# Four edits to an attention-and-FFN kernel: GpSimd operations in pieces, a tensor_reduce for the sums, an earlier hash at the seams, one transposed copy in four on VectorE

## The chip, the cores and the metric

The kernel runs on one core of a Trainium2 chip. Its engines are TensorE (PE in the profile, with weight loads shown apart as PEld), VectorE (DVE), ScalarE (ACT), GpSimd (POOL) and SyncE (SP, which here only issues DMAs). The metric is the device time of one execution in microseconds (us), lower is better.

## The reference

Four batches of eight heads, 768 positions, 64 features per head, all in 32-bit floats. Positions attend only to positions in the same hash bucket; the result goes through an FFN with a three-tap convolution and a gate.

```python
q_bits = (np.einsum('bhsd,dk->bhsk', q, proj) > 0)        # 6 bits; k_bits likewise
mask = q_bucket[:, :, :, None] == k_bucket[:, :, None, :]
scores = np.where(mask, scale * np.matmul(q, k.transpose(0, 1, 3, 2)), -1e9)
attn = np.exp(scores - max)
attn = attn / (np.sum(attn, axis=-1, keepdims=True) + 1e-09)
x = np.matmul(attn, v)                                    # heads side by side: 512 features
h = np.maximum(x @ w_in, 0.0)                             # 1024 features
gate = 1.0 / (1.0 + np.exp(-conv3(h, conv_w)))
out = h * gate @ w_out
```

## The kernel before, in words

**Units.** Two heads make a pair; 4 batches give 16 pairs. A pair has 12 units, each one head's block of 128 queries, in three blocks `qb` of four units (two query tiles `tq` times two heads `h`). The main loop runs over the units `i` and writes out, for every engine, the work of unit `i` and of older units; each engine then runs its own instructions strictly in that order.

**One turn of the loop.** TensorE makes the scores `s` of unit i (`products`, L286). VectorE takes them from PSUM with the row maximum into `e` (`maximum`, L299) and makes `st` (L303). TensorE transposes the exponentials of unit i-3 into `t` (L329), and ScalarE copies them to `at` (`to_sbuf`, L336) and then does the exponential of unit i (L306). `s`, `t` and the hash share three PSUM slots in turn; so the transposes of unit i-1, which come two turns after its scores do, in turn i+2, wait until the maximum of unit i+1 has read its slot.

**The burst.** Every fourth turn, TensorE also does the 24 matmuls of attention times values of an older block (`v`, L355). In that same turn VectorE scales the block before it (`x`, L364), GpSimd splits that into a high part `xh` (L365) and a low part `xl` (L366), and both take their share of the background work below. In the first six pairs the softmax is normalised after the values, by factors `rec` made from four row sums (`reciprocals`: 1e-9 added at L320, reciprocal at L321, spread at L323). In later pairs GpSimd normalises `e` directly (L314).

**Background work, in the first six pairs.** The weights arrive as 64-bit floats. VectorE decodes 16 blocks of 512 columns with four instructions each: L95, L97 (`upper`), L102, L104 (`lower`). ScalarE rounds the result (L136), and GpSimd makes the low part in `ends` (L139, L140). At each burst 3.75 such VectorE steps are written out. The decoded block lies in one of two buffers `wu`, so L97 of a block waits for the `ends` (L140) of the block two before it.

**Preparing the next pair.** Queries and keys of a pair arrive in one buffer `R`. `split` makes the high part `hi` (L204) and the low part in place (L209, called lo below) and sends both out by DMAs; `hash` multiplies `R` by the projection on TensorE (L219), VectorE makes bits (L222), GpSimd scales them (L224). `prepare` cuts this into seven steps; from the second unit of a pair on, one step is taken per turn. `R` of the pair after the next is loaded at a pair's eighth unit, when its last low part has been sent.

**The FFN.** A batch's FFN runs two pairs after its attention. The turns in which the last block of such a pair is transposed are called `ending`; at the last of them the whole FFN is written out (`ffn`: matmuls `h` L393 and `o` L423, VectorE L402 and L406, GpSimd L412), and it takes prepare's steps from its fourth step on. This place is called the seam; there are three with a pair still to be prepared.

Of the kernel before, what the change touches and what calls it, by code (L numbers as in the profile page):

```python
# [7 lines left out]
F32 = mybir.dt.float32  # L8
# [4 lines left out]
ALU = mybir.AluOpType  # L13

B, H, S, D = 4, 8, 768, 64
NB = 6
DM, DFF = 512, 1024
P = 128
NP = H // 2
NCK = S // P  # L20
HS = S // 2
QB = 256
# [15 lines left out]
W0 = 7  # L38
RATE = 3.75
WC = 512  # L40


@with_exitstack
def lsh_attention_conv_ffn(ctx, tc, qk, v, hw, w_in, conv_w, w_out, consts, ident_in, out):
    nc = tc.nc
    PSUM = bass.MemoryType.PSUM
    cp = ctx.enter_context(tc.tile_pool(name="const", bufs=1))
    wp = ctx.enter_context(tc.tile_pool(name="work", bufs=1))
# [4 lines left out]
    def ring(pool, bufs, shape, dtype, tag, name):  # L53

        k = turns[tag] = (turns.get(tag, -1) + 1) % bufs
        return pool.tile(shape, dtype, tag=f"{tag}{k}", name=name, bufs=1)
# [8 lines left out]
    nc.scalar.dma_start(cst, consts)  # L65

    weights = {}

    Q2s = [cp.tile([96, 2, S], F32R, name=f"q2_{i}") for i in range(2)]
    K2s = [cp.tile([96, 2, S], F32R, name=f"k2_{i}") for i in range(2)]  # L70
# [3 lines left out]
    class Decode:  # L74
# [4 lines left out]
        def __init__(self, raw, n, name):  # L79
            pr, self.name = raw.rearrange("p (n two) -> p n two", two=2), name  # L80
            self.lo, self.hi = pr[:, :, 0].bitcast(U32), pr[:, :, 1]
            self.up, self.low = (ring(wp, bufs, [P, WC], I32, f"w{x}", f"w{x}{name}")[:, :n]
                                for x, bufs in (("u", 2), ("l", 5)))
# [23 lines left out]
    def split_weights():  # L107

        todo, ends = [], None

        def ahead():
            if fetched:
                raw, name = fetched.pop(0)
                todo.append(Decode(raw, WC, name))
                todo[-1].size()

        ahead()  # L120
        ahead()
        yield
        for d in todo:
            d.clamp()
        yield
        while todo:
            d = todo.pop(0)
            ahead()
            yield from d.upper()
            if ends:  # L130
                ends()
            if len(todo) == 2:
                todo[-1].clamp()
            yield from d.lower()
            blk = weights[d.name] = cp.tile([P, 2, WC], F32R, tag=f"w{d.name}", name=f"w{d.name}")
            nc.scalar.copy(blk[:, 0, :], d.upf)  # L136

            def ends(d=d, blk=blk):
                nc.gpsimd.tensor_tensor(d.upf, d.upf, blk[:, 0, :].bitcast(F32), ALU.subtract)  # L139
                nc.gpsimd.tensor_tensor(blk[:, 1, :], d.upf, d.lowf, ALU.add)  # L140

        ends()

    def decode_taps(raw):
# [32 lines left out]
    class Pair:  # L177
# [22 lines left out]
        def split(self, h):  # L200

            lo, R = self.R[:, h], self.R[:, h].bitcast(F32)
            hi = ring(wp, 1, [P, S], F32R, "hi", f"hi{self.nm}_{h}")
            nc.gpsimd.tensor_scalar(hi, R, 1.0, 0.0, ALU.mult, ALU.add)  # L204
            for dst, src in ((self.Q1[:64, h], hi[:64]), (self.Q2[:64, h], hi[:64]),
                             (self.K1[:64, h], hi[64:]), (self.K1[64:, h], hi[64:])):
                nc.sync.dma_start(dst.bitcast(F32), src.bitcast(F32))
            yield
            nc.gpsimd.tensor_tensor(lo, R, hi.bitcast(F32), ALU.subtract)  # L209
            for dst, src in ((self.Q1[64:, h], lo[:64]), (self.K2[:64, h], lo[64:])):  # L210
                nc.sync.dma_start(dst.bitcast(F32), src.bitcast(F32))

# [61 lines left out]
    class Unit:  # L274
# [14 lines left out]
        def maximum(self, prev):  # L289

            self.st = ring(wp, 8, [P, 4], F32, "st", f"st{self.nm}")
            pr = self.pair
            if self.tq == 0 and self.h == 0 and not pr.late:
                pr.sums = ring(wp, 3, [P, QB // P, 2], F32, "sums", f"sums{self.nm}")
            self.sums = None if pr.late else pr.sums
            self.sum = self.st[:, 2:3] if pr.late else pr.sums[:, self.tq, self.h:self.h + 1]
            e = wp.tile([P, 776], F32, tag="e", name=f"e{self.nm}", bufs=EB)
            self.e = e[:, :S]
            nc.vector.tensor_scalar(self.e.rearrange("p (a b) -> p a b", a=2), self.sp[:, :, :HS],  # L299
                                    MASKED, None, ALU.max, ALU.max, accum_out=self.st[:, 0:1])  # L300
            if prev and prev.pair.late:
                prev.total()
            nc.vector.tensor_scalar(self.st[:, 1:2], self.st[:, 0:1], -SCALE, None, ALU.mult)  # L303
# [12 lines left out]
        def reciprocals(self):  # L316

            pr = self.pair
            sums = self.sums
            nc.vector.tensor_scalar(sums, sums, 1e-9, None, ALU.add)  # L320
            nc.vector.reciprocal(sums, sums)  # L321
            pr.rec = ring(wp, 1, [P, QB // P, 2, D], F32, "rec", f"rec{self.nm}")
            nc.gpsimd.tensor_scalar(pr.rec, sums.unsqueeze(3).to_broadcast([P, QB // P, 2, D]), 1.0, 0.0,  # L323
                                    ALU.mult, ALU.add)

        def transposes(self):
# [5 lines left out]
        def to_sbuf(self):  # L332
            pr = self.pair
            if self.tq == 0 and self.h == 0:
                pr.at = [ring(wp, 4, [P, 2, 3, QB], F32, "big", f"at{pr.nm}_{self.qb}_{hh}") for hh in range(2)]
            nc.scalar.copy(pr.at[self.h][:, :, :, self.tq * P:(self.tq + 1) * P],  # L336
                           self.tp[:, :, :3 * P].rearrange("p j (c q) -> p j c q", c=3))

    def values(pr, qb, ats, rec):

# [41 lines left out]
    g2, prep = [None], [iter(())]  # L382
# [94 lines left out]
    n = len(units)  # L477
    ffn_after = {min((b + 1) * NP - 1 + DEFER, B * NP - 1): b for b in range(B)}
    for i in range(n + LAG):
        u = units[i] if i < n else None  # L480
        w = units[i - LAG] if i >= LAG else None
        prev = units[i - 1] if 1 <= i <= n else None
        pi, k = divmod(i, 2 * NCK)
        burst = AVS[(i - LAG) % 4] > 0
        for high, low in outs:
            high()
        lows, outs = lows + outs, []
        wi = (i - LAG) // (2 * NCK)
        ending = w and wi in ffn_after and w.qb == S // QB - 1
        if u:  # L490
            u.products()
        if ending:
            for high, low in lows:
                low()
            lows = []
        if u:
            u.maximum(prev)
        elif prev and prev.pair.late:
            prev.total()
        two = units[i - 2] if 2 <= i <= n + 1 else None  # L500
        if two and not two.pair.late and two.tq == QB // P - 1 and two.h == 1:
            two.reciprocals()
        if w and w is not early:
            w.transposes()
            w.to_sbuf()
        if u:
            u.exponential()
        if prev and prev.pair.late:
            prev.normalise()
        if i in (0, 2):  # L510
            next(first, None)
        if burst:
            for high, low in lows:
                low()
            lows = []
        if u and k == PREP and pi + 1 < len(pairs):
            prep[0] = pairs[pi + 1].prepare()
        next(prep[0], None)
        for _ in range(1 + NCK if ending else AVS[(i - LAG) % 4]):
            if av:  # L520
                steps, last = av[0]
                steps.pop(0)()
                if not steps:
                    outs.append(last)
                    av.pop(0)
        if burst and i >= W0:
            background(RATE)
        if u and k == PREP + PREP_N and pi + 1 < len(pairs):
            pairs[pi + 1].load_v()
            if pi + 2 < len(pairs):  # L530
                pairs[pi + 2].load()
        if i == 3:
            taps.append(decode_taps(cwr))
        for g in taps:
            next(g, None)
        fetch(i % 2 if i < 8 else burst)
        if w and w.tq == QB // P - 1 and w.h == 1:
            if not ending:
                av.append(values(w.pair, w.qb, w.pair.at, w.pair.rec))
            else:  # L540
                def fill():
                    steps, last = values(w.pair, w.qb, w.pair.at, w.pair.rec)
                    for step in [*steps, *last]:
                        step()

                bi = ffn_after[wi]
                early = units[i + 1 - LAG] if i + 1 - LAG < n else None

                def transposes_ahead():
                    if early:  # L550
                        early.transposes()
                        early.to_sbuf()
                        turns["S"] -= 1

                ffn(bi, [pairs[bi * NP + c].x for c in range(NCC)], fill, transposes_ahead)
# [43 lines left out]
```

## Time and profile before

| | |
|---|---|
| median of 3 runs | 749.99 us (748.79 to 753.88) |
| profiled execution, its own time | 750.76 us |
| its span in the trace | 749.0 us |
| mean granted TensorE clock | 0.984 of full speed |
| busy share: PE, DVE, ACT, POOL | 95%, 67%, 68%, 50% |

Busy shares are means over the whole span. In the rows of the profile the columns are: line, engine, operation, out<-in with sizes, count, then busy time, mean duration, and the idle time ahead with what ended it. A timeline row begins with start and duration; the idle time before it stands in brackets.

### The profile page before, as it was taken

What the parts mean: (1) busy time and instruction counts of PE and PEld (TensorE: products, weight loads), DVE (VectorE), ACT (ScalarE), POOL (GpSimd) and SP (SyncE); (2) the same over time, 40 slices, a digit from 0 to 9 for tenths busy, and PEclk for the clock granted to TensorE, in tenths of its full rate; (3) what the DMA queues carried; (4) which work ended last, traced back from release to release, by engine and by line L of the source; (5) the groups of instructions that cost most, each with busy time, mean ns of one, the idle gap of its engine ahead of it and who ended that gap; (6) DMA issues with size and microseconds to landing.
All of it is one profiled execution on the core that took longest, in us unless ns stands there. A gap on an engine that the chain in (4) does not pass through costs nothing.

```text
span 749.0 us, 13385 instructions
## 1 busy us (share of the span) xinstructions
PE 714.4 (95%) x4588; PEld 587.5 (78%) x4588; DVE 499.2 (67%) x1195; ACT 509.2 (68%) x954; POOL 373.6 (50%) x372
## 2 busy tenths in 40 slices
PE   5989999988899999999999999999999999999997
PEld 3767777776679987777788988777788897778986
DVE  7588999977667656666657655665666665564663
ACT  5867887886655548778774557787785547785554
POOL 4366777756566324755735423656645323341221
PEclk8999999998999999999999999999999999999999
DMA  3876576553412102365441302255461211000011
GB/s 141 198 204 155 141 206 181 168 162 85 114 43 72 64 37 70 82 181 136 121 121 31 104 1 105 68 150 132 119 163 33 70 43 63 2 1 1 0 43 43
DMA packets 30357, 72.18 MB, mean 96 GB/s; under 512 B 5937, under 2 KB 7505, under 8 KB 30289
## 3 DMA queue, kind: packets, MB, share of 16 engines
q1 hardware_dynamic: 27696, 62.88, 30.9%
q10 hardware_dynamic: 2592, 8.44, 3.6%
q8 instruction: 37, 0.61, 0.3%
q14 instruction: 32, 0.25, 0.1%
HBM read 27.40 MB, written 6.29 MB: 45 GB/s over the span
## 4 chain that ended last, share of the span: by engine, by line
PE 69%; DVE 4%; POOL 4%; DMA 3%; ACT 1%; issue 1%; SPq 0%; POOLq 0%; DVEq 0%
PE o L423 18%; PE h L393 17%; PE s L286 11%; PE t L329 11%; PE v L355 11%; DVE e L299 2%; DMA k<-R 1%; DMA R<-in_qk 1%; PE hash L219 1%; POOL wuo L139 1%; POOL e L314 1%; POOL wo L140 1%; ACT e L306 1%; DVE wuo L97 1%; POOL R L209 1%
## 5 line engine op out<-in xcount | busy, mean ns | idle before, releaser
L299 DVE TENSOR_SCALAR_CACHE_REDUCE e<-s 128x768 f32<-128x768 f32 x192 | 183.3, 955 | 80.9 <-PE s L286 72.1
L306 ACT ACTIVATE e<-e,st 128x768 f32<-128x768 f32 x192 | 181.2, 944 | 23.1 <-DVE st L303 12.8
L336 ACT COPY at<-t 128x768 f32<-128x768 f32 x192 | 152.3, 794 | 47.3 <-PE t L329 47.1
L329 PE MATMUL t<-ident,e 128*128 128x128 f32 x1152 | 164.5, 280 | 19.9 <-DVE e L299 17.9
L314 POOL TENSOR_SCALAR e<-e,st 128x768 f32<-128x768 f32 x120 | 109.3, 911 | 117.3 <-ACT at L336 59.9
L329 PEld LDWEIGHTS t<-ident,e 128*128 128x128 f32 x1152 | 133.4, 144 | 42.6 <-DVE e L299 22.4
L402 DVE SCALAR_TENSOR_TENSOR ht<-ht,cw 128x384 f32<-128x384 f32 (+1 forms) x128 | 117.8, 921 | 70.0 <-ACT ht L400 66.8
L412 POOL TENSOR_TENSOR g<-ht,g 128x384 fp32r<-128x384 f32 x64 | 72.0, 1125 | 163.9 <-ACT g L411 129.7
L423 PE MATMUL o<-wo,g 128*128 128x512 f32 x576 | 143.3, 395 | 0.7 <-POOL g L412 0.7
L393 PE MATMUL h<-xh,wi 128*128 128x386 f32 x512 | 142.0, 340 | 0.0
L355 PE MATMUL v<-at,v 128*64 128x256 f32 x1152 | 134.9, 383 | 0.0
L423 PEld LDWEIGHTS o<-wo,g 128*128 128x128 f32 x576 | 107.0, 188 | 23.5 <-ACT ht L400 1.2
L286 PE MATMUL s<-K,Q 128*128 128x384 f32 x384 | 118.7, 391 | 1.0 <-POOL K L253 0.9
L355 PEld LDWEIGHTS v<-at,v 128*64 128x64 f32 x1152 | 78.7, 137 | 45.5 <-issue 10.9
L286 PE MATMUL s<-k,q 96*128 96x384 f32 x384 | 102.2, 348 | 2.2 <-DVE e L299 2.2
L405 ACT ACTIVATE ht<-ht 128x384 f32<-128x384 f32 x64 | 33.6, 525 | 96.4 <-DVE ht L402 96.4
L393 PEld LDWEIGHTS h<-xh,wi 128*128 128x128 f32 x512 | 94.0, 188 | 3.7 <-ACT ht L400 1.2
L393 PE MATMUL h<-xl,wi 128*128 128x386 f32 x256 | 86.8, 339 | 0.0
L286 PEld LDWEIGHTS s<-K,Q 128*128 128x128 f32 x384 | 60.1, 196 | 22.2 <-issue 17.4
L286 PEld LDWEIGHTS s<-k,q 96*128 96x128 f32 x384 | 72.9, 197 | 3.0 <-ACT q L266 3.0
L406 DVE TENSOR_TENSOR ht<-ht 128x384 f32<-128x384 f32 x64 | 41.5, 649 | 31.5 <-ACT ht L405 31.3
L209 POOL TENSOR_TENSOR R<-R,hi 128x768 fp32r<-128x768 f32 x30 | 60.4, 2014 | 0.9 <-PE hash L219 0.8
(75 smaller groups left out, 622.2 us busy)
## 6 DMA issues: line engine op xcount, KB each, us to landing
R<-in_qk SPq DMA_DIRECT2D x15, 768.0 KB
K<-hi SPq DMA_DIRECT2D x60, 192.0 KB
v<-in_v SPq DMA_DIRECT2D x16, 384.0 KB
out<-osb SPq DMA_DIRECT2D x24, 256.0 KB
Q<-hi SPq DMA_DIRECT2D x30, 192.0 KB
q<-hi SPq DMA_DIRECT2D x30, 192.0 KB
Q<-R SPq DMA_DIRECT2D x30, 192.0 KB
k<-R SPq DMA_DIRECT2D x30, 192.0 KB
```

The costliest lines, as they stand in the source:

```text
L209: nc.gpsimd.tensor_tensor(lo, R, hi.bitcast(F32), ALU.subtract)
L286: nc.tensor.matmul(self.sp[:, half, :HS], A[:, h, qs], C[:, h, half * HS:(half + 1) * HS], start=(kk == 0), stop=(kk == 1))
L299: nc.vector.tensor_scalar(self.e.rearrange("p (a b) -> p a b", a=2), self.sp[:, :, :HS], MASKED, None, ALU.max, ALU.max, accum_out=self.st ...
L306: nc.scalar.activation(self.e, self.e, AF.Exp, bias=self.st[:, 1:2], scale=SCALE, accum_out=self.sum)
L314: nc.gpsimd.tensor_scalar(self.e, self.e, self.st[:, 3:4], 0.0, ALU.mult, ALU.add)
L329: nc.tensor.transpose(self.tp[:, c // 3, c % 3 * P:(c % 3 + 1) * P], self.e[:, c * P:(c + 1) * P], ident)
L336: nc.scalar.copy(pr.at[self.h][:, :, :, self.tq * P:(self.tq + 1) * P], self.tp[:, :, :3 * P].rearrange("p j (c q) -> p j c q", c=3))
L355: nc.tensor.matmul(av[h * D:(h + 1) * D, :QB], vt[:, c, h, :], ats[h][:, c // 3, c % 3, :], start=(c == 0), stop=(c == NCK - 1), tile_posi ...
L393: nc.tensor.matmul(hp[:, :HW], w, x[:, c0:c0 + HW], start=(n == 0), stop=(n == 3 * NCC - 1))
L402: nc.vector.scalar_tensor_tensor(t[:, a:z], ht[:, o + k - 1 + a:o + k - 1 + z], cw[:, f, k:k + 1], t[:, a:z], ALU.mult, ALU.add)
L412: nc.gpsimd.tensor_tensor(g[:, 1, :], t, g[:, 0, :].bitcast(F32), ALU.subtract)
L423: nc.tensor.matmul(op, l, r, start=(f == 0 and n == 0), stop=(f == NFC - 1 and n == 2))
```

## The change

- **Pieces.** GpSimd's lo (L209) and both instructions of `ends` (L139, L140) are done in pieces of 256 columns, `hi` (L204) in pieces of 384.
- **Sums.** The three buffers of row sums have a second column that GpSimd fills with 1e-9 once at the start. A `tensor_reduce` over the two columns takes the place of the addition at L320.
- **Seam.** In `ending` turns a second step of `prepare` is taken.
- **Copy.** The copy to `at` for the first unit of each block (one in four) is done by VectorE; the others stay on ScalarE.

```diff
+PC = 256
+def pieces(n, step):
+    return [slice(c, c + step) for c in range(0, n, step)]
...
+    sums4 = [cp.tile([P, 2 * QB // P, 2], F32, name=f"sums{i}") for i in range(3)]
+    for t in sums4:
+        nc.gpsimd.memset(t, 1e-9)
...
             def ends(d=d, blk=blk):
-                nc.gpsimd.tensor_tensor(d.upf, d.upf, blk[:, 0, :].bitcast(F32), ALU.subtract)
-                nc.gpsimd.tensor_tensor(blk[:, 1, :], d.upf, d.lowf, ALU.add)
+                for c in pieces(WC, PC):
+                    nc.gpsimd.tensor_tensor(d.upf[:, c], d.upf[:, c], blk[:, 0, c].bitcast(F32), ALU.subtract)
+                for c in pieces(WC, PC):
+                    nc.gpsimd.tensor_tensor(blk[:, 1, c], d.upf[:, c], d.lowf[:, c], ALU.add)
...
-            nc.gpsimd.tensor_scalar(hi, R, 1.0, 0.0, ALU.mult, ALU.add)
+            for c in pieces(S, HS):
+                nc.gpsimd.tensor_scalar(hi[:, c], R[:, c], 1.0, 0.0, ALU.mult, ALU.add)
...
-            nc.gpsimd.tensor_tensor(lo, R, hi.bitcast(F32), ALU.subtract)
+            for c in pieces(S, PC):
+                nc.gpsimd.tensor_tensor(lo[:, c], R[:, c], hi[:, c].bitcast(F32), ALU.subtract)
...
-                pr.sums = ring(wp, 3, [P, QB // P, 2], F32, "sums", f"sums{self.nm}")
+                pr.sums = sums4[self.qb % 3]
...
-            self.sum = self.st[:, 2:3] if pr.late else pr.sums[:, self.tq, self.h:self.h + 1]
+            self.sum = self.st[:, 2:3] if pr.late else pr.sums[:, 2 * self.tq + self.h, 0:1]
...
-            nc.vector.tensor_scalar(sums, sums, 1e-9, None, ALU.add)
-            nc.vector.reciprocal(sums, sums)
+            inv = ring(wp, 2, [P, QB // P, 2], F32, "inv", f"inv{self.nm}")
+            nc.vector.tensor_reduce(inv.rearrange("p t h -> p (t h)"), sums, mybir.AxisListType.X, ALU.add)
+            nc.vector.reciprocal(inv, inv)
...
-            nc.scalar.copy(pr.at[self.h][:, :, :, self.tq * P:(self.tq + 1) * P],
-                           self.tp[:, :, :3 * P].rearrange("p j (c q) -> p j c q", c=3))
+            copy = nc.vector.tensor_copy if self.tq == 0 and self.h == 0 else nc.scalar.copy
+            copy(pr.at[self.h][:, :, :, self.tq * P:(self.tq + 1) * P],
+                 self.tp[:, :, :3 * P].rearrange("p j (c q) -> p j c q", c=3))
...
         next(prep[0], None)
+        if ending:
+            next(prep[0], None)
```

Line numbers move, so the rows of the change carry other numbers than those of before (L299 becomes L312, L364 becomes L380, L95 to L104 become L104 to L113, L139 and L140 become L149 and L151, L209 becomes L222, L219 becomes L232).

VectorE in a burst of the third pair, before (maximum of unit i, its `st`, `x`, four decode steps, maximum of unit i+1):

```order
L299 TENSOR_SCALAR e_2_3_1_1051,st_2_3_1_1050<-s_2_3_1_1045 128x768
L303 TENSOR_SCALAR st_2_3_1_1050<-st_2_3_1_1050 128x1
L364 TENSOR_TENSOR x_1_2_1065<-v_1_2_902,rs_1_2_903 128x256
L95 TENSOR_SCALAR wli_1_717<-wli_1_717 128x512
L97 SCALAR_TENSOR_TENSOR wui_1_716<-rawi_1_586,wli_1_717 128x512
L102 TENSOR_SCALAR wli_1_717<-wui_1_716 128x512
L104 SCALAR_TENSOR_TENSOR wli_1_717<-rawi_1_586,wli_1_717 128x512
L299 TENSOR_SCALAR e_2_4_0_1114,st_2_4_0_1112<-s_2_4_0_1107 128x768
```

And the same place of the changed kernel:

```order
L312 TENSOR_SCALAR e_2_3_1_1080,st_2_3_1_1079<-s_2_3_1_1074 128x768
L316 TENSOR_SCALAR st_2_3_1_1079<-st_2_3_1_1079 128x1
L352 COPY at_2_1_0_1090<-t_2_2_0_1083 128x6x128
L380 TENSOR_TENSOR x_1_2_1094<-v_1_2_926,rs_1_2_927 128x256
L104 TENSOR_SCALAR wli_1_738<-wli_1_738 128x512
L106 SCALAR_TENSOR_TENSOR wui_1_737<-rawi_1_602,wli_1_738 128x512
L111 TENSOR_SCALAR wli_1_738<-wui_1_737 128x512
L113 SCALAR_TENSOR_TENSOR wli_1_738<-rawi_1_602,wli_1_738 128x512
L312 TENSOR_SCALAR e_2_4_0_1146,st_2_4_0_1145<-s_2_4_0_1140 128x768
```

The copy to `at` now stands in VectorE's queue in the burst's turn, ahead of `x`, the decode steps and the next maximum.

GpSimd in the burst of the sixth pair near 184 us, before:

```order
L365 TENSOR_SCALAR xh_0_1808<-x_0_2_2208 128x256
L366 TENSOR_TENSOR xl_0_1809<-x_0_2_2208,xh_0_1808 128x256
L209 TENSOR_TENSOR R_2_1863<-R_2_1863,hi_2_1_2160 128x768
L139 TENSOR_TENSOR wuo_1722<-wuo_1722,wo_2102 128x512
L140 TENSOR_TENSOR wo_2102<-wuo_1722,wlo_1723 128x512
```

And now:

```order
L381 TENSOR_SCALAR xh_0_1861<-x_0_2_2271 128x256
L382 TENSOR_TENSOR xl_0_1862<-x_0_2_2271,xh_0_1861 128x256
L222 TENSOR_TENSOR R_2_1918<-R_2_1918,hi_2_1_2222 128x256 x3
L149 TENSOR_TENSOR wuo_1772<-wuo_1772,wo_2164 128x256 x2
L151 TENSOR_TENSOR wo_2164<-wuo_1772,wlo_1773 128x256 x2
```

The order is the same; three instructions have become seven.

TensorE at the second seam, before (last scores and transposes ahead of the FFN, first FFN matmuls; the hash stood sixty rows further on, ahead of the first `o`):

```order
L286 MATMUL s_2_0_1_4328<-k_0_75,q_0_73 128x384 x2
L329 MATMUL t_1_5_1_4338<-ident,e_1_5_1_4249 128x128 x6
L393 MATMUL h_0_0_4350<-xh_0_1808,wi_0_450 128x386
L393 MATMUL h_0_0_4350<-xl_0_1809,wi_0_450 128x386
L393 MATMUL h_0_0_4350<-xh_0_1808,wi_0_450 128x386
```

And now:

```order
L299 MATMUL s_2_0_1_4427<-k_0_81,q_0_79 128x384 x2
L343 MATMUL t_1_5_1_4437<-ident,e_1_5_1_4347 128x128 x6
L232 MATMUL hash_3_4448<-R_3_4271,hw_sb 32x384 x4
L409 MATMUL h_0_0_4470<-xh_0_1861,wi_0_461 128x386
L409 MATMUL h_0_0_4470<-xl_0_1862,wi_0_461 128x386
```

The hash of the next pair has moved ahead of the FFN's first matmul.

More of the change, by code (lines that the diff above doesn't have):

```diff
@@ L319, in reciprocals @@
             sums = self.sums
-            nc.vector.tensor_scalar(sums, sums, 1e-9, None, ALU.add)
-            nc.vector.reciprocal(sums, sums)
+            inv = ring(wp, 2, [P, QB // P, 2], F32, "inv", f"inv{self.nm}")
+            nc.vector.tensor_reduce(inv.rearrange("p t h -> p (t h)"), sums, mybir.AxisListType.X, ALU.add)
+            nc.vector.reciprocal(inv, inv)
             pr.rec = ring(wp, 1, [P, QB // P, 2, D], F32, "rec", f"rec{self.nm}")
-            nc.gpsimd.tensor_scalar(pr.rec, sums.unsqueeze(3).to_broadcast([P, QB // P, 2, D]), 1.0, 0.0,
+            nc.gpsimd.tensor_scalar(pr.rec, inv.unsqueeze(3).to_broadcast([P, QB // P, 2, D]), 1.0, 0.0,
                                     ALU.mult, ALU.add)
```

## The prediction

> **What bounds the kernel now.** The page comes first, then the busy times by stage, then TensorE's waits in each stage.
>
> ```profile
> span 749.0 us, 13385 instructions
> PE 714.4 (95%) x4588; PEld 587.5 (78%) x4588; DVE 499.2 (67%) x1195; ACT 509.2 (68%) x954; POOL 373.6 (50%) x372
> ```
> ```profile
> 24.70:155.00 130.30, 119.30 (x873) 93.81 (x872) 112.22 (x240) 102.16 (x191) 90.02 (x91) 0.97 0.63 173
> 155.00:204.90 49.90, 41.81 (x281) 33.80 (x280) 34.66 (x85) 32.78 (x61) 28.55 (x31) 0.90 0.46 127
> 204.90:749.00 544.10, 536.32 (x3353) 448.51 (x3351) 332.59 (x835) 357.97 (x679) 244.18 (x236) 1.00 0.26 72
> ```
> ```profile
> PE t L329 <- DVE e L299: 9.8, 9, 2.3
> ...
> PE t L329 <- DVE e L299: 8.1, 4, 3.5
> ```
>
> TensorE is busy 95% of the span. The stage rows give, from the left, length, then PE, PEld, DVE, ACT, POOL busy, then granted clock. From 204.9 us on TensorE is busy 536.3 of 544.1 us at full clock: whatever VectorE, ScalarE and GpSimd save there buys nothing, while a new wait of TensorE there is paid in full. Before that, two stages leave it idle, nearly all of it in the waits below them: transposes wait for a maximum on VectorE, nine times (9.8 us) up to 155 us, four times (8.1 us) up to 204.9. The clock there is below one, so idle time costs twice; what is lost to it is about 0.03 x 130.3 = 3.9 and 0.10 x 49.9 = 5.0 us. So 26.8 us is all that the first 205 us could give, start-up aside.
>
> **The first stage: why the maximum is late.** One burst, on three engines:
>
> ```profile
> 90.84 0.42 DVE L364 TENSOR_TENSOR x<-v,rs 128x256 f32<-128x256 f32 x1
> 91.19 0.42 DVE L95 TENSOR_SCALAR wli<-wli 128x512 int32<-128x512 int32 x1
> ...
> 92.44 0.84 DVE L102 TENSOR_SCALAR wli<-wui 128x512 int32<-128x512 int32 x1
> 93.31 2.20 DVE L104 SCALAR_TENSOR_TENSOR wli<-rawi,wli 128x512 f32<-128x512 uint32 x1
> 95.44 0.94 DVE L299 TENSOR_SCALAR_CACHE_REDUCE e<-s 128x768 f32<-128x768 f32 x1
> ```
> ```profile
> 91.95 1.05 POOL L366 TENSOR_TENSOR xl<-x,xh 128x256 fp32r<-128x256 f32 x1
> 92.96 2.01 POOL L209 TENSOR_TENSOR R<-R,hi 128x768 fp32r<-128x768 f32 x1
> ```
> ```profile
> 90.53 2.81 PE L355 MATMUL v<-at,v 128*64 128x256 f32 x24
> ...
> 96.45 0.88 PE L329 MATMUL t<-ident,e 128*128 128x128 f32 x6 [0.86 <-DVE e L299]
> ```
> ```profile
> L102 DVE TENSOR_SCALAR wli<-wui x8: 474/829/1952, 38.8 to 113.6; 128x512 int32<-128x512 int32 x8
> ...
> L104 DVE SCALAR_TENSOR_TENSOR wli<-rawi,wli x8: 694/1126/2203, 39.3 to 120.3; 128x512 f32<-128x512 uint32 x8
> ...
> L209 POOL TENSOR_TENSOR R<-R,hi x30: 1813/1999/2395, 19.0 to 587.0; 128x768 fp32r<-128x768 f32 x30
> ...
> L366 POOL TENSOR_TENSOR xl<-x,xh x18: 729/786/1715, 39.1 to 212.5; 128x256 fp32r<-128x256 f32 x18
> ...
> L429 DVE COPY osb<-o x8: 677/685/692, 251.8 to 744.7; 128x512 f32<-128x512 f32 x8
> ```
>
> L104 starts 0.35 us after lo (L209) and ends 0.5 us after it. The rows by line (shortest, median, longest in ns) say the same: L104 takes 694 undisturbed and 2,203 at worst, L102 474 and 1,952. So a decode step that meets a long GpSimd operation waits until that ends. The queue from `x` to the next maximum decides TensorE's gap: here 95.44 - 91.19 = 4.25 us of decode for a gap of 0.86, so some 3.4 us of decode pass unseen.
>
> **Copy, cost.** VectorE's copy from PSUM of 512 columns takes 0.685 us. `x`, with one operand in PSUM and 256 columns, takes 0.42, so 256 more columns add about 0.27: 0.95 for 768, less the 0.07 by which VectorE's instructions overlap in the rows above (90.84 + 0.42 against 91.19): **0.9 us**. It stands between the maximum and `x`, in the queue that decides the gap. ScalarE's saved copy frees nothing that TensorE waits for. The stage has thirteen bursts and nine gaps. Eight gap bursts pay 0.9 each, 7.2. The first gap is VectorE waiting for GpSimd, which hides the copy but not the pieces ahead of it (0.6):
>
> ```profile
> 29.75 0.82 DVE L95 TENSOR_SCALAR wli<-wli 128x512 int32<-128x512 int32 x1 [4.62 <-POOL wli L90]
> ```
>
> Four bursts without a gap have some slack; I take half, 2.0. Sum 9.8; the ends are 7.8 and 11.4.
>
> **Pieces, gain.** Lo stands beside the decode in two of three bursts of a pair, eight here. A step that now waits up to 1.5 us for it (2,203 - 694) would wait for a piece of 256 columns, 0.73 by L366: 0.8 saved. The step after it meets a piece of `ends` in place of a whole one in about half the cases, 0.5 less: 1.05 a burst, **8.4 us**. The ends: 0, if GpSimd's next piece goes ahead of the waiting step, and 2.1 a burst, 16.8, if no step waits at all. I take the middle, since in the burst above the two engines took turns (L104 waited for lo, not for the `ends` behind it). Net for the stage **+1.4**. One gap, the longest (2.3), should fall to about 1.5 and keep its clock: **-1.7** by the price below.
>
> **The second stage: GpSimd's chain.** Near 184 us the next maximum waits behind L97, which waits for L140:
>
> ```profile
> DVE wuo L97 <- POOL wo L140: 8.0, 3, 4.3
> ```
> ```profile
> 190.73 0.69 DVE L97 SCALAR_TENSOR_TENSOR wuo<-rawo,wlo 128x512 int32<-128x512 int32 x1 [4.29 <-POOL wo L140]
> ```
> ```profile
> 184.48 0.52 POOL L365 TENSOR_SCALAR xh<-x 128x256 fp32r<-128x256 f32 x1 [3.16 <-DVE x L364]
> ...
> 186.12 2.00 POOL L209 TENSOR_TENSOR R<-R,hi 128x768 fp32r<-128x768 f32 x1
> 188.08 1.28 POOL L139 TENSOR_TENSOR wuo<-wuo,wo 128x512 f32<-128x512 f32 x1
> 189.44 1.26 POOL L140 TENSOR_TENSOR wo<-wuo,wlo 128x512 fp32r<-128x512 f32 x1
> ```
> ```profile
> 192.35 0.87 PE L329 MATMUL t<-ident,e 128*128 128x128 f32 x6 [3.54 <-DVE e L299]
> ```
>
> All of GpSimd's chain starts from `x`, and `x` now stands behind the copy: +0.9. Here pieces only add fixed time. Three pieces of lo take 3 x 0.73 less two overlaps of 0.04, 2.11 against 1.81: +0.3. Four pieces of `ends` take 4 x 0.73 - 0.12 = 2.8 against 2.62 (188.08 to 190.70): +0.2. Three such waits, two of them with lo: 2 x 1.4 + 1.1, **+3.8 us**; the ends are 1.1 (copy hidden) and 6.
>
> **The seams: a new wait.** The hash reads `R`, and moves from the FFN's fourth step to a place ahead of its first matmul. SP loads `R`, and GpSimd's `hi` waits for the same load:
>
> ```profile
> 379.71 0.82 PE L329 MATMUL t<-ident,e 128*128 128x128 f32 x6
> 380.28 0.42 PE L393 MATMUL h<-xh,wi 128*128 128x386 f32 x1
> ```
> ```profile
> 377.76 0.39 SPq L191 DMA_DIRECT2D R<-in_qk  x1
> ...
> 552.51 0.39 SPq L191 DMA_DIRECT2D R<-in_qk  x1
> ```
> ```profile
> 382.43 0.83 POOL L204 TENSOR_SCALAR hi<-R 128x768 fp32r<-128x768 f32 x1 [1.44 <-DMA R<-in_qk]
> ```
> ```profile
> 554.71 0.42 PE L393 MATMUL h<-xh,wi 128*128 128x386 f32 x1
> ```
> ```profile
> 557.11 0.83 POOL L204 TENSOR_SCALAR hi<-R 128x768 fp32r<-128x768 f32 x1 [1.70 <-PE h L393]
> ```
>
> At the second seam TensorE would reach the hash at 380.28, and `R` lands at 382.43; at the third 554.71 and, after the same 4.6 us from the issue, 557.11. In TensorE's queue everything of the FFN stands behind it: gaps of 2.15 and 2.40, **+4.55 us**, in a stage without slack. At the first seam `R` is long there. The hash's own matmuls are only moved. VectorE's bits, GpSimd's lo and bits and their DMAs on SP come earlier, where these engines have idle time in the FFN; what they leave free later was not waited for. A gap also costs clock:
>
> ```profile
> 192.30:197.40 5.10, 5.05 (x27) 4.92 (x28) 3.42 (x11) 4.22 (x8) 1.61 (x4) 0.67 0.52 167
> 86.70:90.30 3.60, 3.52 (x27) 3.48 (x28) 3.25 (x12) 3.30 (x7) 2.68 (x5) 1.00 0.14 39
> ```
> ```profile
> 86.78 0.88 PE L329 MATMUL t<-ident,e 128*128 128x128 f32 x6 [1.54 <-DVE e L299]
> ```
>
> The same 27 matmuls take 5.05 us after the gap of 3.54 and 3.52 after one of 1.54: 1.6 lost. A mean clock of 0.97 in the first stage, whose longest gap is 2.3, says that gaps near two are enough. Two seams: **+3.3**, the ends 0 and 3.3. [...]
>
> **Edits at nothing.** The `tensor_reduce` takes the place of a tiny addition two turns after a burst, where VectorE has time left. The three fills precede GpSimd's first input. Past 205 us the copy lies under TensorE's 2.8 us of values. Without that cover it would cost 0.9 for each of some thirty bursts, 27 us; nothing in the rows points there.
>
> **Sum.** 1.4 - 1.7 + 3.8 + 4.55 + 3.3 = +11.35 on the profiled execution's 750.76 gives 762.1. The median before, 749.99, lies 0.8 below that execution: **761 us**. What can be told from no change is 1%, 7.5 us.
>
> **The rivals.**
> - *The clock holds at the seams.* The gate lets gaps of two us pass, and only longer ones, as that of 3.54, cost clock. 761 - 3.3 = 757.7, half of it within 1%. For it: no row shows the clock behind one such gap alone. Against it: the 0.97. Chance 0.15. [...]
> - *Pieces give VectorE no turn.* If the next piece goes ahead of a waiting decode step, the 8.4 and the 1.7 are gone: 771. For it: a piece starts as soon as the last one ends. Against: the turns taken in the burst above. Chance 0.13, slower.
> - *The blocking ends altogether.* Place: the decode steps of the first two stages. If they never wait, and GpSimd is not held up by them, all 26.8 us go, against 7.85 for the seams: 731, faster. It decides once 7.85 + 7.5 = 15.4 of the 26.8 are gone. Against it: 8.1 + 5.0 hang on L140, which pieces don't shorten. Chance 0.10. A half-way case, 745 to 753, has 0.12. It is also what remains if the seam's wait is not there.
>
> **How the numbers follow.** The forecast, 755 to 768, has 0.50, of which 0.06 lie below the 1% line. Slower by over 1%: 0.44 + 0.07 + 0.13 = 0.64; within 1%: 0.06 + 0.08 + 0.12 = 0.26; faster 0.10. The range leaves out the 0.10 of the faster case and a little at each end: 750 to 771.
>
> **What would show it.** Right: hash waiting for DMA `R` at about 382 and 557 us, two TensorE gaps of two us and a clock below one behind them; no decode step above 1.4 us; 48 copies near 0.95 on VectorE; larger gaps between 160 and 192 us. Wrong: gaps of the first stage gone, or a load of `R` that lands before the seam.

## The result: 11 us slower

The changed kernel takes 762.17 us (median of four runs, 760.39 to 762.63). The kernel before, on the same chip, takes 749.39 (four runs, 746.30 to 753.88). The ratio is 1.0149, with an interval of 1.0114 to 1.0184, so about 11.2 us slower. (The two medians are 12.8 us apart; their quotient, 1.0171, lies inside the interval.) The forecast was 761 in a range of 750 to 771, with slower by over 1% as the likeliest sign. The sum was right. What it was made of was right in part only, as the experiments show.

**The profile after.** The first two lines of the page, then the stage rows (length, then PE, PEld, DVE, ACT and POOL busy, granted clock) of the same two stretches as before:

```profile
span 760.2 us, 13531 instructions
...
PE 717.5 (94%) x4588; PEld 592.0 (78%) x4588; DVE 521.4 (69%) x1243; ACT 478.0 (63%) x906; POOL 390.3 (51%) x497
```
```profile
24.70:155.00 130.30, 119.86 (x884) 93.81 (x883) 112.46 (x258) 94.90 (x180) 96.48 (x139) 0.99 0.64 176
155.00:204.90 49.90, 38.20 (x251) 30.84 (x250) 30.93 (x72) 26.48 (x50) 28.86 (x41) 0.86 0.45 119
```

TensorE does about as much in the first stretch as before, at a clock of 0.99 in place of 0.97; in the second it is busy 3.6 us less, at 0.86 in place of 0.90. TensorE's waits (total, times, longest), first from 24.7 to 155 us, then from 155 us on:

```profile
PE v L366 <- POOL rec L337: 3.1, 5, 0.8
PE t L343 <- DVE e L312: 2.4, 5, 0.6
PE t L343 <- ACT at L352: 2.0, 1, 2.0
PE hash L232 <- ACT e L319: 1.8, 1, 1.8
PE s L299 <- ACT at L352: 0.9, 1, 0.9
PE hash L232 <- DMA R<-in_qk: 0.2, 1, 0.2
```
```profile
PE t L343 <- DVE e L312: 12.1, 4, 5.0
PE hash L232 <- DMA R<-in_qk: 4.9, 3, 2.1
```

In the first stage the wait for the maximum, 9.8 us before, is 2.4. In its place TensorE waits for GpSimd's reciprocals (3.1), twice for one of ScalarE's copies to `at` (2.0 and 0.9) and for a load of `R` (1.8; the row names `e`, but GpSimd's `hi` waits for the same load just there). The six rows add up to 10.4 us; before it was 9.8 + 1.0 = 10.8. So the waits have changed their names and hardly their sum. Later the waits for the maximum grew from 8.1 to 12.1, and the seams are new:

```profile
386.58 0.85 PE L232 MATMUL hash<-R,hw_sb 128*32 128x384 f32 x8 [2.08 <-DMA R<-in_qk]
387.36 0.48 PE L409 MATMUL h<-xh,wi 128*128 128x386 f32 x1
387.64 0.53 PE L409 MATMUL h<-xl,wi 128*128 128x386 f32 x1
...
565.00 1.45 PE L232 MATMUL hash<-R,hw_sb 128*32 128x384 f32 x8 [2.13 <-DMA R<-in_qk]
```
```profile
386.58:391.00 4.42, 4.42 (x20) 3.67 (x20) 0.62 (x1) 1.65 (x4) 4.42 (x7) 0.62 0.51 118
565.00:570.00 5.00, 5.00 (x24) 3.45 (x26) 0.62 (x1) 1.78 (x5) 4.53 (x7) 0.66 0.56 133
```

At the second and third seam the hash waits 2.08 and 2.13 us for `R`, and behind it the clock is 0.62 and 0.66: one `h` matmul takes 0.53 us where it takes 0.34 at full clock.

### The profile page after: what moved, and what is told of

The parts are those of the page before. It is cut to its first block, busy times and chain, and to the rows that moved or that the text cites. A ratio compares the mean times of both kernels' runs of the same rounds, so it can differ in the third digit from the quotient of the medians.

```text
span 760.2 us, 13531 instructions
## 1 busy us (share of the span) xinstructions
PE 717.5 (94%) x4588; PEld 592.0 (78%) x4588; DVE 521.4 (69%) x1243; ACT 478.0 (63%) x906; POOL 390.3 (51%) x497
## 4 chain that ended last, share of the span: by engine, by line
PE 72%; DMA 8%; DVE 8%; POOL 7%; ACT 2%; issue 2%; SPq 0%; ACTq 0%; DVEq 0%; POOLq 0%
PE o L439 18%; PE h L409 18%; PE s L299 12%; PE t L343 12%; PE v L371 12%; DMA R<-in_qk 3%; DVE e L312 3%; DMA k<-R 3%; POOL R L222 2%; PE hash L232 1%; ACT e L319 1%; POOL e L327 1%; DMA k<-bits 1%; DMA K<-hi 1%; POOL wuo L149 1%
## 5 line engine op out<-in xcount | busy, mean ns | idle before, releaser
L312 DVE TENSOR_SCALAR_CACHE_REDUCE e<-s 128x768 f32<-128x768 f32 x192 | 183.3, 955 | 61.1 <-PE s L299 53.6
L343 PEld LDWEIGHTS t<-ident,e 128*128 128x128 f32 x1152 | 133.2, 144 | 39.8 <-issue 18.2
L409 PE MATMUL h<-xh,wi 128*128 128x386 f32 x512 | 143.8, 345 | 0.0
L352 ACT COPY at<-t 128x768 f32<-128x768 f32 x144 | 114.0, 793 | 47.4 <-PE t L343 47.1
L299 PE MATMUL s<-K,Q 128*128 128x384 f32 x384 | 118.7, 391 | 1.9 <-POOL K L266 1.0
L371 PEld LDWEIGHTS v<-at,v 128*64 128x64 f32 x1152 | 80.8, 137 | 43.6 <-issue 10.8
L299 PE MATMUL s<-k,q 96*128 96x384 f32 x384 | 101.1, 345 | 2.4 <-ACT q L279 2.3
L409 PEld LDWEIGHTS h<-xh,wi 128*128 128x128 f32 x512 | 95.8, 192 | 6.1 <-issue 4.0
L299 PEld LDWEIGHTS s<-K,Q 128*128 128x128 f32 x384 | 60.0, 196 | 23.5 <-issue 16.2
L299 PEld LDWEIGHTS s<-k,q 96*128 96x128 f32 x384 | 72.1, 195 | 3.2 <-ACT q L279 3.2
L222 POOL TENSOR_TENSOR R<-R,hi 128x256 fp32r<-128x256 f32 x90 | 71.6, 822 | 0.4 <-PE hash L232 0.4
L422 DVE TENSOR_TENSOR ht<-ht 128x384 f32<-128x384 f32 x64 | 39.5, 617 | 32.5 <-ACT ht L421 32.5
```

Of the source, the lines that this page charges most:

```text
L222: nc.gpsimd.tensor_tensor(lo[:, c], R[:, c], hi[:, c].bitcast(F32), ALU.subtract)
L299: nc.tensor.matmul(self.sp[:, half, :HS], A[:, h, qs], C[:, h, half * HS:(half + 1) * HS], start=(kk == 0), stop=(kk == 1))
L343: nc.tensor.transpose(self.tp[:, c // 3, c % 3 * P:(c % 3 + 1) * P], self.e[:, c * P:(c + 1) * P], ident)
L371: nc.tensor.matmul(av[h * D:(h + 1) * D, :QB], vt[:, c, h, :], ats[h][:, c // 3, c % 3, :], start=(c == 0), stop=(c == NCK - 1), tile_posi ...
L409: nc.tensor.matmul(hp[:, :HW], w, x[:, c0:c0 + HW], start=(n == 0), stop=(n == 3 * NCC - 1))
```

## The experiments

Each ratio below is against runs of the kernel before on the same chip; a per cent is 7.5 us. The table shows one profile of each kernel: the time from the first to the thirteenth burst (rows `v<-ident,rec`, 24.45 and 148.63 us before), from there to the first matmul of `h`, and from there to the end of the span.

| kernel | ratio (interval) | bursts 1 to 13 | to first h | rest |
|---|---|---|---|---|
| before | 1 | 124.2 | 56.3 | 544.1 |
| the whole change | 1.0149 (1.0114 to 1.0184) | 122.6 | 62.0 | 550.9 |
| e1, all but the seam | 1.0038 (1.0012 to 1.0065) | 122.1 | 60.6 | 543.5 |
| e2, all but the copy | 1.0028 (1.0008 to 1.0047) | 119.4 | 57.8 | 547.1 |
| e3, copy alone | 1.0161 (1.0128 to 1.0193) | 133.2 | 61.8 | 544.2 |
| e4, pieces alone | 0.9973 (0.9954 to 0.9992) | 119.9 | 58.4 | 544.5 |
| e5, seam alone | 1.0043 (1.0020 to 1.0066) | 121.2 | 57.2 | 546.5 |
| e7, lo in pieces | 0.9963 (0.9940 to 0.9987) | 120.4 | 58.4 | 543.7 |
| e8, ends in pieces | 0.9969 (0.9946 to 0.9992) | 119.5 | 56.4 | 543.2 |
| e9, pieces, hash later | 1.0042 (1.0025 to 1.0060) | 121.8 | 54.1 | 548.9 |
| e10, sums alone | 0.9963 (0.9946 to 0.9979) | 122.6 | 55.2 | 542.6 |
| e11, hash later | 0.9960 (0.9942 to 0.9979) | 119.9 | 54.5 | 546.3 |
| e12, sums, hash later | 0.9893 (0.9858 to 0.9929) | 118.8 | 54.2 | 545.6 |

Up to the first seam e5 issues what before issues, and yet the two profiles differ by 3.0 us in the third column. So a difference of 3 us in one profile's stage is no finding; the ratios decide.

### e1: all but the seam

```diff
         next(prep[0], None)
-        if ending:
-            next(prep[0], None)
```

> The whole change without its seam edit. Theory: the two late loads of R and the clock behind them are worth 4.55 + 3.3 us, so about 754.3 us, and the trace has no hash that waits for the load and full clock from 210 us on. Rival, part of the cost is elsewhere (the earlier lo and bits delay GpSimd's work for the feed-forward part): still above 757, with gaps there. Rival, the clock would have held: 757.7.

Measured: 753.20 us, ratio 1.0038. The quotient of the two ratios, 1.0149 / 1.0038 = 1.0111, makes the seam edit worth 8.3 us within this change (from both intervals, roughly 5 to 12). Around the second seam the stage now runs at full clock without a gap, and so does the stretch from 555 to 575 us around the third:

```profile
380.00:390.00 10.00, 10.00 (x70) 8.37 (x69) 5.37 (x19) 8.34 (x15) 3.70 (x5) 1.00 0.56 155
390.00:400.00 10.00, 10.00 (x57) 8.58 (x56) 6.40 (x9) 5.37 (x11) 3.38 (x4) 1.00 0.03 7
```

The theory holds here, and both rivals fall.

### e5: the seam alone

```diff
         next(prep[0], None)
+        if ending:
+            next(prep[0], None)
```

> The kernel before with the seam edit alone. Theory of the forecast, 2.15 + 2.40 us of waiting and 3.3 of clock whatever comes ahead: about 758.5 us (750.6 + 7.85). Rival, the price hangs on when R happens to land and steps at some length of the gap (without the copy one seam waited 0.78 us and kept its clock, the other 2.03 and lost it): 752 to 756, with at least one seam whose hash waits under 1.5 us and full clock behind it.

Measured: 751.92 us, 3.2 us slower (0.0043 x 749; 1.5 to 4.9 by the interval): the rival, whose 752 to 756 was counted from 750.6. The same edit costs 8.3 in one kernel and 3.2 in the other. The second seam and the clock behind the second and third, in this kernel:

```profile
378.74 0.85 PE L219 MATMUL hash<-R,hw_sb 128*32 128x384 f32 x8 [0.72 <-ACT e L306]
379.52 0.44 PE L393 MATMUL h<-xh,wi 128*128 128x386 f32 x1
379.81 0.33 PE L393 MATMUL h<-xl,wi 128*128 128x386 f32 x1
...
555.04 0.85 PE L219 MATMUL hash<-R,hw_sb 128*32 128x384 f32 x8 [2.09 <-DMA R<-in_qk]
```
```profile
378.74:383.16 4.42, 4.42 (x32) 3.13 (x34) 0.88 (x4) 4.08 (x7) 4.03 (x4) 1.00 0.54 130
555.04:560.04 5.00, 5.00 (x38) 3.54 (x40) 1.11 (x2) 2.68 (x5) 4.08 (x4) 1.00 0.58 139
```

At the second seam the gap is 0.72 us (the row names `e`, but GpSimd's `hi` waits for the load of `R` until the same moment, 378.68 us). At the third it is 2.09, as long as those of the whole change, and the clock stays at 1.00 all the same. Why the second gap is short shows in SP's queue, first in the whole change, then here: the last DMA of the pair before out of `R` (`k<-R`), and the load of the next `R`, which waits until that has landed, since `R` has one buffer.

```profile
376.79 0.83 SPq L224 DMA_DIRECT2D k<-R  x1
...
381.99 0.39 SPq L202 DMA_DIRECT2D R<-in_qk  x1
```
```profile
370.29 0.84 SPq L211 DMA_DIRECT2D k<-R  x1
...
374.39 0.38 SPq L191 DMA_DIRECT2D R<-in_qk  x1
```

From one to the other it takes 5.20 us there and 4.10 here. TensorE reaches the hash 2.51 us after the load's issue there (386.58 - 2.08 - 381.99) and 3.63 after it here (378.74 - 0.72 - 374.39). Counted from the issue of `k<-R` it is there at the same time in both, after 7.71 and 7.73 us. So at the second seam one us in a small DMA makes or unmakes the gap; at the third the gaps are alike, and only the clock differs. Each kernel has one profile here; that their medians differ by the same two causes is likely, but not shown.

### e3: the copy alone

```diff
-            nc.scalar.copy(pr.at[self.h][:, :, :, self.tq * P:(self.tq + 1) * P],
-                           self.tp[:, :, :3 * P].rearrange("p j (c q) -> p j c q", c=3))
+            copy = nc.vector.tensor_copy if self.tq == 0 and self.h == 0 else nc.scalar.copy
+            copy(pr.at[self.h][:, :, :, self.tq * P:(self.tq + 1) * P],
+                 self.tp[:, :, :3 * P].rearrange("p j (c q) -> p j c q", c=3))
```

> The kernel before with the one copy on VectorE and nothing else. Theory: 749.4 + 9.8 + 2.7 = 761.9 us, with transposes that wait some 0.9 us longer for each maximum up to 155 us. Rival, the copy is hidden (it stands where VectorE would have waited for GpSimd anyway): 750 to 753, and the waits for the maximum are as before up to 155 us.

Measured: 762.21 us, ratio 1.0161, or 12.1 us; the theory, which had 12.5. This one edit costs as much as the whole change. TensorE's waits up to 155 us:

```profile
PE t L329 <- DVE e L299: 17.4, 11, 2.4
PE hash L219 <- DMA R<-in_qk: 1.3, 1, 1.3
```

Eleven waits for the maximum in place of nine, 17.4 us in place of 9.8. The bursts take 9.0 us more (133.2 - 124.2).

### e4: the pieces alone

```diff
-            nc.gpsimd.tensor_tensor(lo, R, hi.bitcast(F32), ALU.subtract)
+            for c in pieces(S, PC):
+                nc.gpsimd.tensor_tensor(lo[:, c], R[:, c], hi[:, c].bitcast(F32), ALU.subtract)
```

and `hi` and the ends of the decode likewise.

> The kernel before with GpSimd's hi, lo and the ends of the decode in pieces, and nothing else. Theory: 8.4 us of the waits for the maximum and 1.7 of clock go up to 155 us, 1.1 is added in the three waits behind it: about 740.4 us. Rival, a new wait takes the place (GpSimd's queue is longer by the fixed time of the pieces, so the reciprocals, the freeing of R and with it the next load come later): 746 to 750, with transposes of the first stage that wait for the maximum under 3 us in all but for GpSimd and loads over 4.

Measured: 748.98 us, 2.0 us faster: the rival, on its number. The waits up to 155 us:

```profile
PE hash L228 <- DMA R<-in_qk: 4.6, 3, 1.9
PE t L338 <- DVE e L308: 3.2, 4, 2.2
PE v L359 <- POOL rec L332: 1.1, 2, 0.6
```

The maxima gave back 6.6 us (9.8 - 3.2), as the theory has it, within 1.8. But TensorE, which is earlier, now meets a hash whose `R` has not landed (4.6 in place of 1.0) and reciprocals that GpSimd has not made (1.1). The three rows make 8.9 us, where before had 10.8. (The rival asked for maxima under 3 us; they are at 3.2.) Here is one such load, with the lo ahead of it:

```profile
66.33 0.59 SPq L220 DMA_DIRECT2D k<-R  x1
...
72.05 0.39 SPq L198 DMA_DIRECT2D R<-in_qk  x1
```
```profile
76.49 0.85 PE L228 MATMUL hash<-R,hw_sb 128*32 128x384 f32 x8 [1.53 <-DMA R<-in_qk]
```

The load waits 5.7 us for the lo's DMA and takes 4.4 itself. No step of that loop runs on VectorE, so a faster VectorE does not shorten it.

### e2: all but the copy

```diff
-            copy = nc.vector.tensor_copy if self.tq == 0 and self.h == 0 else nc.scalar.copy
-            copy(pr.at[self.h][:, :, :, self.tq * P:(self.tq + 1) * P],
-                 self.tp[:, :, :3 * P].rearrange("p j (c q) -> p j c q", c=3))
+            nc.scalar.copy(pr.at[self.h][:, :, :, self.tq * P:(self.tq + 1) * P],
+                           self.tp[:, :, :3 * P].rearrange("p j (c q) -> p j c q", c=3))
```

> The whole change with all four copies on ScalarE again. Theory, the copy costs 0.9 us a burst in the queue before the maximum: 9.8 us up to 155 and 2.7 in the three waits behind it go, about 749.7 us. Rival, the copy lay mostly beside waits that stay (GpSimd's reciprocals, the loads of R, ScalarE's copies): only the 2.7 and about 1 us go, about 758.5, and the stage up to 155 us keeps its length within 2 us.

Measured: 752.81 us, ratio 1.0028. So within the change the copy costs 9.0 us (1.0149 / 1.0028 = 1.0121), between the theory's 12.5 and the rival's 3.7, nearer to the theory. Alone it costs 12.1. The intervals of the two overlap, so it is not shown that the copy is cheaper in company; if it is, part of it falls into waits that are there anyway.

### e7 and e8: which pieces

e7 cuts only lo, e8 only the ends of the decode.

> The kernel before with only lo in three pieces; hi and the ends of the decode whole. If lo is what VectorE waits for, as the forecast said for half a wait of 1.5 us in eight bursts, most of the gain of the pieces is here: 748 to 749.5, with the third and fourth decode step at most 1.4 us but for those beside the ends. Rival, the ends count as much: 750.5, with decode steps near 2 us beside them.

> The kernel before with only the ends of the decode in four pieces; hi and lo whole. If lo is what VectorE waits for: 750.5 to 752, the waits for the maximum as before up to 155 us and 0.2 us longer in each of the three waits behind it. Rival, the ends count as much as lo: 749 to 750, with two to four us fewer of waits for the maximum up to 155 us.

Measured: 746.69 (0.9963) and 746.97 (0.9969). Each alone is worth 2.3 to 2.8 us, and both together, with `hi`, 2.0. For lo the gain is above the theory's; for the ends it is on the rival's side, and more. The longest decode step of the `wi` blocks is 1.74 us in e7 and still 2.21 in e8, where lo is whole. TensorE's waits up to 155 us, first e7, then e8:

```profile
PE hash L225 <- DMA R<-in_qk: 3.3, 2, 2.4
PE t L335 <- DVE e L305: 2.2, 3, 1.6
```
```profile
PE t L336 <- DVE e L306: 5.6, 6, 1.2
PE hash L226 <- DMA R<-in_qk: 2.3, 2, 1.8
```

That the two gains do not add up fits the limit that e4 shows: the first cut already brings TensorE to the load of `R` (3.3 and 2.3 us, where before had 1.0).

### e6 and e9: the pieces, with hi and the hash one turn later

```diff
-            for now in ((sa,), (), (hs, sa), (hs,), (sb,), (), (sb,)):
+            for now in ((), (sa,), (sa,), (hs,), (hs, sb), (), (sb,)):
```

(e6; `sa`, `sb` are hi and lo of the pair's two heads, `hs` the hash.) In e6 lo overwrites the first head's half of `R` ahead of the hash, which therefore hashes the remainder of that half; this changes what is computed.

> GpSimd's pieces alone, and the next pair's hi, first lo and hash one turn later (the last steps and the next load where they were). Theory: in the pieces alone the 6.6 us won from the maxima were taken back by R, whose load waits for the lo of the pair before; a turn later R has landed, the 4.6 us of hash waits up to 155 us go to under 1 and the time to 744 to 746. Rival, the loads were no cause but a place where the wait shows (GpSimd is as late as before): the wait moves to the reciprocals or the maxima, 748 to 750.

Measured: 775.70 us, ratio 1.0351 (1.0316 to 1.0386). The hash now waits for GpSimd's lo, ten times and 17.4 us in all, 12.5 of them past 203 us. This says nothing on the late load. e9 keeps the hash ahead of lo:

```diff
+            for now in ((), (sa,), (), (hs, sa), (hs, sb), (), (sb,)):
```

> GpSimd's pieces alone, with hi one turn later and the hash one turn later, still ahead of the lo that overwrites R; the last steps and the next load stay where they were. Theory: with the pieces alone TensorE met a hash whose R had not landed, 4.6 us up to 155 us, since the load waits for the lo of the pair before; one turn later R has landed, those waits go below 1 us and the time to 743 to 746. Rival, the late load only shows where GpSimd is late: the wait moves to the reciprocals or the maxima, 747 to 750.

Measured: 752.39 us, ratio 1.0042: the theory falls, and the rival is not slow enough either. The waits up to 155 us:

```profile
PE v L359 <- POOL rec L332: 6.8, 7, 1.5
PE t L338 <- DVE e L308: 1.3, 2, 0.9
```

No hash waits for `R` any more, as the theory said, and transposes wait little for the maximum. The wait has moved to GpSimd's reciprocals, which stand in its queue behind the pieces; 1.7 us more are waits of scores for the DMAs out of `R`, which now come later. In the rest, after the first `h`, TensorE's transposes wait 4.0 us for the exponentials that GpSimd normalises and its `o` matmuls 1.6 for GpSimd's `g`, where before these rows were 1.8 and 0.7; that makes 3.1 of the 4.8 us that the rest takes more. So GpSimd is the third bound, behind VectorE and the loop of `R`.

### e11: the order alone

```diff
-            for now in ((sa,), (), (hs, sa), (hs,), (sb,), (), (sb,)):
+            for now in ((), (sa,), (), (hs, sa), (hs, sb), (), (sb,)):
```

> The kernel before with only hi and the hash one turn later, nothing in pieces. Theory: before had 1.0 us of hash waits up to 155 us, so at most 1 us goes: 748 to 749.5. Rival, the order itself is a gain (lo no longer lies beside the burst's first decode steps): 744 to 747, with fewer waits for the maximum. Rival, it is a loss (lo meets later decode steps): 751 to 754.

Measured: 746.42 us, ratio 0.9960: the first rival, a gain of 3.0 us from the order itself.

```profile
PE t L329 <- DVE e L299: 3.2, 4, 1.1
PE v L350 <- POOL rec L323: 1.6, 4, 0.6
```

Without any piece the waits for the maximum are down to the 3.2 us of e4. Only the first head's lo stands a turn later, yet in this profile none of the decode steps up to 116 us takes more than 1.27 us, where before the longest took 2.20; one near 118 us still meets a lo (1.94). The pieces and the order are two ways to the same 6.6 us, and together (e9) they cost.

### e10 and e12: the sums, and the best version

e10 is the kernel before with the three fills, the `tensor_reduce` and its own tile alone; e12 adds e11's order to it.

```diff
-            nc.vector.tensor_scalar(sums, sums, 1e-9, None, ALU.add)
-            nc.vector.reciprocal(sums, sums)
+            inv = ring(wp, 2, [P, QB // P, 2], F32, "inv", f"inv{self.nm}")
+            nc.vector.tensor_reduce(inv.rearrange("p t h -> p (t h)"), sums, mybir.AxisListType.X, ALU.add)
+            nc.vector.reciprocal(inv, inv)
```

> The kernel before with the tensor_reduce, its three fills and its own tile for the reciprocals, and nothing else. Theory (costed at nothing): 749 to 750, within the interval of no change. Rival: the fills on GpSimd at the start or the reduce between two maxima cost 0.5 to 1.5 us: 750 to 751, with a first hash or a first reciprocal that starts later by as much.

Measured: 746.48 us, ratio 0.9963 (0.9946 to 0.9979): faster by 2.8 us, which neither theory had. The instructions don't explain all of it: the eighteen additions of before take 4.8 us together (157 to 570 ns each), the eighteen reduces of the changed kernel 2.7 (148 to 153), so at most 2.1 us. Its profile has the same waits (9.4 us for the maximum, 1.8 for `R`) and a higher clock, 0.99 and 0.93 against 0.97 and 0.90. But e5, which up to the first seam issues what before issues, shows 1.00 and 0.90 there, so the clock of one profile does not explain the gain either. Its cause stays open.

> The two edits that were each worth 2.7 us alone, together: the tensor_reduce with its fills, and hi and the hash one turn later; nothing in pieces, no copy on VectorE, no seam edit. Theory A, they act on different waits (the reduce on which gaps lose the clock, the order on the waits for the maximum up to 155 us): they add up, 743 to 744.5. Theory B, both only remove the same lost clock of the first 205 us, or the wait moves on to GpSimd's reciprocals as it did with pieces: 745.5 to 748.

Measured: 743.67 us, ratio 0.9893 (0.9858 to 0.9929), faster than both kernels. The two gains add up (0.9963 x 0.9960 = 0.9923 lies in the interval): theory A by its sum. That the sums act on the clock, as theory A has it, is not shown.

## Why the prediction came out as it did

**The copy: right, and within 0.4 us alone** (9.8 + 2.7 forecast, 12.1 measured), as 0.9 us in the queue ahead of the maximum. Its 48 instructions have the forecast duration:

```profile
L352 DVE COPY at<-t x48: 946/948/958, 18.8 to 680.8; 128x768 f32<-128x768 f32 x48
```

Past 205 us it is hidden, as forecast: the rest takes 544.2 us with the copy and 544.1 without.

**The pieces, blocking: right.** The third and fourth decode step of the `wi` blocks (shortest, median, longest in ns) after:

```profile
L111 DVE TENSOR_SCALAR wli<-wui x8: 508/836/841, 39.6 to 111.4; 128x512 int32<-128x512 int32 x8
...
L113 DVE SCALAR_TENSOR_TENSOR wli<-rawi,wli x8: 680/1102/1107, 40.2 to 119.0; 128x512 f32<-128x512 uint32 x8
```

The longest are 841 and 1,107 where they were 1,952 and 2,203, and the longest of any decode step after is 1,225, below the 1.4 us that the forecast named. The engines take turns at a piece's end, as in the burst near 92 us:

```profile
92.01 2.73 POOL L222 TENSOR_TENSOR R<-R,hi 128x256 fp32r<-128x256 f32 x3
```
```profile
92.37 1.11 DVE L113 SCALAR_TENSOR_TENSOR wli<-rawi,wli 128x512 f32<-128x512 uint32 x1
```

The three pieces of lo take 2.73 us here and 2.10 near 388 us, where no decode step is beside them: 0.63 longer, close to the 0.68 that L113 takes undisturbed. The first piece takes 0.91 us and ends at 92.92, L113 ends at 93.48, and the second piece takes 1.17 us, where the third takes 0.71: L113 waited for the first piece, and the second piece for L113. Why one engine waits for the other is not shown. With shorter instructions the longest wait is shorter: L113 takes at most 0.43 us over its shortest (1,107 - 680), where L104 took 1.51 (2,203 - 694).

**The pieces, size: the step that failed.** "1.05 a burst, 8.4 us" (and 1.7 of clock) holds only where VectorE's queue is the last to be ready. Behind the copy it nearly is: from e3 to e1 the bursts shrink by 133.2 - 122.1 = 11.1 us in these two profiles, and the ratios (1.0161 / 1.0038 = 1.0123) give 9.2 us, the edit of the sums (2.8 alone) included. Without the copy it isn't: e4 is 2.0 us faster in all, where 8.4 + 1.7 - 1.1 = 9.0 were forecast. The forecast asked what is late next for the decode steps, and not what is late next for TensorE. It had no term for the loop of `R` and none for the reciprocals, though this row of before, up to 155 us, already showed that `R` can be the last to arrive:

```profile
PE hash L219 <- DMA R<-in_qk: 1.0, 1, 1.0
```

In the changed kernel the copy's cost and the pieces' gain offset each other as forecast (+1.4 - 1.7 = -0.3; the bursts 122.6 - 124.2 = -1.6, within the scatter of one profile). But they did so with other waits than said: the forecast's own sign of error, "gaps of the first stage gone", half came true, since the gaps behind the maximum went and others came.

**The second stage: mechanism right, a little small.** Forecast +3.8; the waits for the maximum grew by 4.0, and the stretch to the first `h` by 62.0 - 56.3 = 5.7, of which 0.8 is the hash, now ahead of `h`. What is left, about one us, is the clock: from the thirteenth burst to the first `h` TensorE is busy 49.8 us in place of 48.2, of which the hash is 0.8, at 0.89 in place of 0.91. The forecast didn't price that. The copy is the larger part, as forecast: alone it adds 5.5 here, the pieces alone 2.1 (the scatter applies).

**The seams: right here, and not a property of the edit.** Forecast 4.55 + 3.3 = 7.85; by e1 it is 8.3, with gaps of 2.08 and 2.13. But e5 shows 3.2 for the same edit. The arrival of `R` was taken from one profile of before, where the DMA ahead of the load took 4.97 us (377.76 less the issue of its last DMA, below); over the thirteen profiles besides e6 it takes 3.98 to 5.33 us at the second seam and 5.15 to 5.43 at the third, so the price of the second seam is a range.

```profile
372.79 0.84 SPq L211 DMA_DIRECT2D k<-R  x1
```

**The clock behind the seams: right, by luck in part.** The forecast took the loss at two us as near certain and gave the rival, for which such a gap costs no clock, 0.15. The profile of before does show the clock behind one such gap alone: 0.68 in the 3 us behind the gap of 2.29 at 55.46 us. Gaps of 2.08 and 2.13 lost it, and one of 2.03 at e2's third seam; one of 2.09 (e5) did not. Over thirteen profiles a gap of 1.74 to 2.49 us lost it 22 times in 37 (below).

**Edits at nothing: wrong by 2.8 us** for the sums (e10), with an open cause. The total of the single edits, 12.1 + 3.2 - 2.0 - 2.8 = 10.5, is near the measured 11.2, though hardly any edit has the same worth alone and in company.

**The sum: close, by luck in part.** In company the copy is worth 9.0 us (e2; forecast 12.5) and the seam edit 8.3 (e1; forecast 7.85). That leaves 11.2 - 9.0 - 8.3 = -6.1 for pieces and sums together, where the forecast had -9.0. Each of these has an interval of some 3 us either way; as they stand, two terms that are each some 3 us too large cancel. Two slips of the working matter little: 5.05 - 3.52 is 1.5 and not 1.6, and 2 x 1.4 + 1.1 is 3.9 and not 3.8.

## What to carry to other kernels

A gain on an engine that others wait for lasts only until the next thing is late: before pricing it, list for the same instruction of TensorE the second and third releaser (here the loop of one buffer, DMA out, load in; then GpSimd's queue), and cap the gain there. An operation moved onto the engine at the end of the queue was paid here at its full duration, while moving a colliding operation by one turn costs no instruction and was worth as much as cutting it up. Where a wait is the difference of two times of a few us, one of them a DMA's landing, price it as a range and not from one profile.

## What the runs showed of the hardware

The clock after a gap is not a matter of length alone. Over the thirteen profiles besides e6, I took every wait of TensorE of a us or more from 20 us on that the profile names, and the mean granted clock of the 3 us behind it. Of 29 waits of 1.01 to 1.57 us none was followed by a clock below 0.95; of 37 between 1.74 and 2.49, 22 were; of 11 between 2.92 and 3.41, 9; of 14 from 3.54 to 4.96, all. So equal gaps end differently, as those of 2.08 and 2.13 us at the seams of the whole change, which lost the clock, and the one of 2.09 in e5, which did not; why is not shown. Around two us it was a toss of a coin, and each loss cost, by estimate, 1.5 us (5.05 - 3.52, the 27 matmuls of the forecast) to 2 us (half of 8.3 - 4.21, the two seams).

Also unexpected: a DMA of the same shape (`k<-R`) took between 3.98 and 5.33 us at the same place of thirteen profiles, from its issue to the issue of the load that waits for it, and that was enough to make or unmake a gap of two us on TensorE.
